# A softcap attention and maxout kernel whose list of work is put in another order

## The chip, the cores and the metric

The kernel runs on one core of one Trainium2 chip. The metric is device time in microseconds (us). Before the change the median of three runs was 328.67 us, the lowest 328.39 and the highest 329.13.

## The reference

Attention with a soft cap on the scores, then a feed-forward layer whose activation is the larger of two products. Inputs and output are float32; batch 8, 12 heads, 448 positions, head size 64, so x has 3584 rows and 768 columns; the hidden width is 1024.

```
scores = scale * (q @ k.T)                 # scale = 1/8
scores = cap * tanh(scores / cap)          # cap = 30
attn   = softmax(scores)
x      = (attn @ v)  -> [3584, 768]
g      = maximum(x @ w1, x @ w2)           # [3584, 1024]
out    = g @ w_out                         # [3584, 768]
```

## The kernel before

**The algebra.** Since max(a, b) = relu(a - b) + b, the kernel forms wd = w1 - w2 (`subtract`, into `wd_sb`) and wm = w2 @ w_out (`turn_w2` and `premultiply`, into `wm_sb`), and computes out = relu(x @ wd) @ w_out + x @ wm. The exponent is taken without subtracting the maximum, which the cap bounds.

**The tiling.** Two heads make a pair i (48 of them), two pairs a quad t (24). Scores are made transposed, three tiles of 128 key positions per pair (`S i j`, two matmuls of 448 columns, one for each head, on 64 rows of the array), and the last 64 positions of all four heads of a quad together (`L t`). ScalarE makes tanh out of PSUM (`T`, `TL`, line 519 and 532) and then exp in SBUF (`E`, `EL`). DVE adds the tiles of exponentials (`A`, `B`); a matmul with ones makes the sums (`Y`), DVE turns and inverts them (`Y1` to `Y3`); `VL` and `V` are the products with v (32-column tiles, four at a time), `N` scales them into xT on DVE.

The layer after it is cut into 120 groups, each of one PSUM bank out of four: per batch eight groups x @ wd of six units of 448 columns (stage 1), and six or eight groups of the output, of 14 units of 384 columns (stage 2). Each unit has two halves of 64 rows, and `M x y n` runs n units of the row half 0 of group x beside row half 1 of group y: two different groups are in work at a time. `ev g` empties a bank on DVE (line 666 for stage 1, 702 for stage 2), `eva g` on ScalarE (line 700); `st` stores rows of the output from SyncE's queue.

**Hand-overs.** Where a group's next matmul is on the other row half than its last, both write the same bank. `H g` (DVE) or `Hs g` (SyncE) issues a nop that waits for the group's last matmul (line 654); the first matmul of the other half then waits for this nop. A change of half with no such step of its own gets no added dependency (lines 634 to 650).

**The loads.** q, k and v of later pairs come through the DMA queue that GpSimd (POOL) feeds, which casts to bf16. `lk i part` and `lq i` fill `kqs` (line 328), `lv t part` fills `vp` and `vl` (line 352). There are two buffers of each, so a load for quad t waits until the buffer of quad t-2 is free: for `kqs` until its transposition has landed, for `vp` and `vl` until the products `V` and `VL` of that quad have read them. For the first ten pairs TensorE transposes q and k (`X`, `Xh`, copied by `XC`, `XCh`); for quads 5 to 23 a DMA transposition on SyncE's queue does (`cr t`, line 475, into `qkT`, also two buffers). The first two pairs come in float32 on the queues of SyncE and ScalarE (`ld0`) and are cast there (`cd`). `lw1`, `lw2`, `lwo` load the weights, on POOL's queue too. `D bank n` are matmuls on constants that keep TensorE at work while nothing else is there.

**What sets the order.** No scheduler: one string, `ORDER` (lines 9 to 202), names every step, and the program issues them one after the other through the table `STEPS`. Each engine and each DMA queue takes its own steps in this order; semaphores carry the dependencies between them. So `ORDER` decides, for TensorE, ScalarE, DVE, POOL's queue and SyncE's queue at once, what stands behind what: a POOL load whose buffer is not free holds every load behind it, and an `Hs` stands behind a `cr` on SyncE if the list says so.

Of the kernel before, what the change touches and what calls it, by code (L numbers as in the profile page):

```python
# [9 lines left out]
ld0 q; ld0 q 1; cd q; ld0 k; ld0 k 1; ms; dm; ms0; cd k; id; lq 2 0; lk 3 0; lq 3 0; lk 2 0; lw2 3; lw2 2; D 3 24;  # L10
Xh 0 0 0; Xh 0 1; cd k 1 1; cd q 1 1; XCh 0 1; XCh 0 0; D 3 4; X 1 1; S 0 0; S 0 1; XC 1; T 0 0; T 0 1; D 0 5;
D 1 8; D 3 1; D 1 4; S 0 2; D 1 4; L 0; D 1 16; T 0 2; TL 0; E 0 0 3; D 1 12; S 1 2; S 1 0; X 3 3; X 2 0; W 3 2;
W 2 1; T 1 0; T 1 2; lw2 1; lwo 0 0; lwo 0 1; lw2 0; lq 4 0; lk 4 0; lv 0 0; lv 0 1; XC 3; XC 2; WC 3; D 0 4;
S 1 1; D 0 8; D 2 2; S 2 1; W 1 2; WC 2; WC 1; T 1 1; T 2 1; S 2 0; D 0 4; L 1; OP 3 0 0; P 3 0 2; OP 1 0 1;
P 1 0 4; P 3 0 2; OP 2 0 3; P 2 0 7; P 1 0 1; P 2 0 1; P 1 0 1; P 3 0 2; P 1 0 2; PC 2 0; PC 1 0; E 1 2 3;
E 1 0 2; TL 1; T 2 0; EL 0; S 3 0; S 2 2; P 3 0 1; W 0 2; P 3 0 1; X 4 3; T 2 2; T 3 0; VL 0; Y 0 1; V 0 0 0 3;
V 0 1 0 3; S 3 1; lwo 1 0; lwo 1 1; lq 5 0; lk 5 0; lv 1 0; lv 1 1; lk 8 0; lq 8 0; lq 7 0; lw2 4; lv 6 2; lq 6 0;
lk 7 0; lk 6 0; lw2 5; lw1 2; lw1 4; lw1 0; lv 2 0; lv 2 1; WC 0; PC 3 0; XC 4; Y1 0; Y2 0; Y3 0; N 0 0; N 0 1;
E 2 0 3; T 3 1; EL 1; E 3 0 2; OP 0 0 1; P 0 0 2; OP 2 1 2; P 2 1 2; P 0 0 1; OP 1 1 3; P 1 1 2; P 0 0 1; P 1 1 2;
P 0 0 1; P 1 1 4; S 4 0; S 3 2; X 5 0; P 2 1 4; P 0 0 3; P 2 1 1; XC 5; PC 1 1; PC 0 0; T 3 2; T 4 0; E 3 2 3;  # L20
OP 3 1 3; P 3 1 1; P 2 1 1; S 4 1; S 4 2; Y 1 1; T 4 1; T 4 2; L 2; P 3 1 4; VL 1; TL 2; V 1 1 0 3; V 1 0 0 3;
S 5 0; X 6 0; E 4 0 3; T 5 0; EL 2; Y1 1; Y2 1; PC 2 1; Y3 1; N 1 1; N 1 0; XC 6; X 7 2; W 4 1; S 5 2; S 5 1;
X 8 0; P 3 1 3; WC 4; XC 8; PC 3 1; T 5 1; T 5 2; OP 4 0 1; P 4 0 2; OP 0 1 0; P 0 1 3; S 6 0; S 6 1; W 5 3;
P 0 1 1; P 4 0 6; P 0 1 4; E 5 0 2; T 6 1; T 6 0; E 5 2 3; XC 7; sub 2 0; WC 5; sub 4 0; PC 4 0; sub 0 0; PC 0 1;
OP 5 1 3; P 5 1 4; S 6 2; L 3; Y 2 1; T 6 2; TL 3; E 6 0 3; VL 2; V 2 1 0 1; V 2 0 0 3; V 2 1 1 3; S 7 0; P 5 1 4;
OP 5 0 0; P 5 0 8; Y1 2; Y2 2; Y3 2; N 2 0; N 2 1; A 3 0 1; A 3 0 2; PC 5 1; PC 5 0; T 7 0; EL 3; lk 9 0; lq 11 0;
lv 3 1; lq 9 0; lw1 1; lw1 3; lq 10 0; lk 12 1; lv 3 0; lw1 5; lk 10 0; lk 11 0; lk 11 1; lk 10 1; S 7 2; O 0 1;
M 0 -1 2; S 7 1; M 0 -1 4; O 1 2; M 1 -1 1; T 7 2; T 7 1; Hs 0; M 1 -1 1; S 8 1; M 1 -1 1; M 1 0 3; S 8 0; X 9 3;
OP 4 1 0; P 4 1 4; sub 1 0; sub 3 0; XC 9; T 8 1; E 7 0 2; T 8 0; E 7 2 3; P 4 1 4; L 4; O 2 3; M 2 0 3; S 8 2;
M 2 1 3; A 3 1 1; B 3 1; PC 4 1; ev 0; B 3 0; Hs 2; TL 4; T 8 2; O 3 0; M 3 1 3; M 3 2 1; S 9 0; M 3 2 2; T 9 0;  # L30
E 8 0 3; ev 1; A 3 1 2; sub 5 0; cr 5; Hs 3; O 4 1; M 4 2 1; VL 3; V 3 0 0 3; Y 3 2; V 3 1 0 3; M 4 2 2; S 9 1;
M 4 3 3; lk 13 0; lk 13 1; lv 4 1; lv 4 0; lv 5 3; lv 5 0; lq 13 0; lq 15 0; lq 12 0; lk 12 0; lk 15 1; Y1 3;
Y2 3; Y3 3; ev 2; Hs 4; O 5 2; M 5 3 3; M 5 4 3; T 9 1; EL 4; ev 3; N 3 0; N 3 1; Hs 5; O 6 3; M 6 4 3; M 6 5 2;
S 10 0; M 6 5 1; O 7 0; M 7 5 3; Hs 6; ev 4; A 4 0 1; ev 5; M 7 6 2; S 9 2; M 7 6 1; Hs 7; cr 6; E 9 0 2; T 10 0;
T 9 2; O 8 1; M 8 6 3; S 10 2; M 8 7 3; S 10 1; O 9 2; M 9 7 1; T 10 2; T 10 1; E 9 2 3; M 9 7 2; VL 4; V 4 0 0 2;
L 5; TL 5; A 4 1 1; H 8; A 4 0 2; B 4 1; ev 7; B 4 0; A 4 1 2; ev 6; M 9 8 3; V 4 1 0 3; Y 4 0; V 4 0 2 3;
# [169 lines left out]
def kernel(  # L206
# [21 lines left out]
    P = 128  # L228
# [550 lines left out]
```

## Time and profile before

| what | value |
|---|---|
| median of the runs | 328.67 us |
| span of the profiled execution | 326.9 us |
| TensorE busy | 320.2 us, 98% |
| ScalarE busy | 281.1 us, 86% |
| DVE busy | 240.1 us, 73% |
| POOL busy | 162.2 us, 50% |
| matmuls | 4138 |
| longest single waits of POOL's loads: for a transposition / for scores of TensorE | 6.3 us / 9.5 us |

The profile is of one execution, and its span stands 1.8 us under the median of the runs, which contains what lies around it. PE is TensorE, PEld its loading of weights, ACT ScalarE, DVE VectorE, SP SyncE; a q behind the name means the engine's queue of instructions. The share of busy time is a mean over unlike stages: a head of about 56 us in which the weights are prepared and the first quads start, a long middle, and a tail from about 286 us in which only groups of the last batches remain. In the slices each digit is the busy share of one fortieth of the span, in tenths.

### The profile page before, as it was taken

Reading aid. Unit: us, or ns where it says so; the run is one execution under the profiler, and the core shown is the slowest. Engines: PE = TensorE matmul, PEld = TensorE weight load, DVE = VectorE, ACT = ScalarE, POOL = GpSimd, SP = SyncE. Lnnn points to the kernel's source line nnn. Section 1 sums busy time; section 2 is a strip of 40 time slices with the busy share of each in tenths; the row PEclk is TensorE's granted clock in tenths of the full one; section 3 lists DMA queues with packets and bytes.
Section 4 is the critical chain, followed back from the end, with each engine's and each line's share of the span. In section 5 each row is a group of like instructions: output and inputs, shape, how many; then the busy total and the mean of one; then the engine's idle time right before and its main releaser. Section 6 shows DMA issues by size and latency. Waiting matters only on the chain.

```text
span 326.9 us, 9772 instructions
## 1 busy us (share of the span) xinstructions
PE 320.2 (98%) x4138; PEld 184.5 (56%) x4138; DVE 240.1 (73%) x422; ACT 281.1 (86%) x278; POOL 162.2 (50%) x237
## 2 busy tenths in 40 slices
PE   7999999999999999999999999999999999999994
PEld 3454545545656664565565565556466556557662
DVE  3346899987997778987897788968878779773201
ACT  5999999999999999999999999999999999921120
POOL 7357584568772772764774474478448311000000
PEclk9999999999999999999999999999999999999999
DMA  8999999899999999999999999999999963013033
GB/s 179 174 202 185 269 256 112 92 140 116 221 188 98 134 182 191 102 99 175 163 176 108 208 114 181 128 140 182 183 116 101 201 156 45 2 50 98 0 98 96
DMA packets 134508, 46.28 MB, mean 142 GB/s; under 512 B 112321, under 2 KB 129473, under 8 KB 134465
## 3 DMA queue, kind: packets, MB, share of 16 engines
q0 software_dynamic: 94592, 25.02, 78.3%
q1 hardware_dynamic: 39424, 19.99, 31.1%
q8 instruction: 32, 0.52, 0.6%
q10 hardware_dynamic: 448, 0.66, 0.5%
q14 instruction: 12, 0.09, 0.1%
HBM read 47.78 MB, written 11.01 MB: 180 GB/s over the span
## 4 chain that ended last, share of the span: by engine, by line
PE 93%; DMA 3%; POOL 1%; DVE 1%; issue 0%
PE mm L645 61%; PE s L514 9%; PE s L606 9%; PE mm L431 5%; DMA w2b<-in_moe_w_dram 3%; PE s L528 2%; PE s L600 2%; PE mm L573 2%; PE mm L640 1%; POOL kqs L321 1%; PE mm L458 1%; PE mm L566 1%; PE mm L416 0%; DVE xT L621 0%; POOL w2b L366 0%; DVE xT L618 0%
## 5 line engine op out<-in xcount | busy, mean ns | idle before, releaser
L519 ACT ACTIVATE e<-s 128x896 bf16<-128x896 f32 x144 | 125.5, 927 | 5.7 <-PE s L514 5.2
L536 ACT ACTIVATE e<-e 128x1792 bf16<-128x1792 bf16 (+2 forms) x72 | 122.7, 1709 | 0.0
L645 PE MATMUL mm<-wo_sb,gT 64*128 64x384 bf16 x864 | 115.2, 323 | 0.0
L645 PE MATMUL mm<-wm_sb,xT 64*128 64x384 bf16 x648 | 102.2, 323 | 0.0
L645 PE MATMUL mm<-xT,wd_sb 64*128 64x448 bf16 x768 | 97.5, 349 | 0.0
L328 POOL DMA_DIRECT2D kqs<-in_k_dram x76 | 54.7, 722 | 56.1 <-DMA qkT<-kqs 50.9
L645 PEld LDWEIGHTS <-gT 64*128 64x128 bf16 x864 | 58.6, 94 | 25.5 <-issue 1.1
L645 PEld LDWEIGHTS <-wd_sb 64*128 64x128 bf16 x768 | 48.8, 94 | 26.7 <-issue 2.1
L645 PEld LDWEIGHTS <-xT 64*128 64x128 bf16 x648 | 50.3, 94 | 18.5 <-issue 0.2
L514 PE MATMUL s<-qkT 64*128 64x448 bf16 x288 | 52.7, 352 | 0.2 <-DVE xT L618 0.2
L352 POOL DMA_DIRECT2D vp<-in_v_dram x48 | 30.5, 639 | 32.6 <-PE s L514 23.5
L666 DVE TENSOR_SCALAR gT<-mm 128x448 bf16<-128x448 f32 x64 | 38.9, 617 | 8.7 <-PE mm L645 7.6
L328 POOL DMA_DIRECT2D kqs<-in_q_dram x38 | 35.1, 924 | 5.7 <-issue 2.5
L606 PE MATMUL s<-e,vp 128*32 128x448 bf16 x576 | 36.1, 354 | 0.0
L548 DVE TENSOR_TENSOR esum<-e 128x896 bf16<-128x896 bf16 x42 | 25.9, 617 | 9.1 <-ACT e L536 9.1
L621 DVE TENSOR_TENSOR xT<-s,inv 64x448 bf16<-64x448 f32 x48 | 29.9, 622 | 1.7 <-PE s L606 0.8
L548 DVE TENSOR_TENSOR esum<-esum,e 128x896 bf16<-128x896 bf16 x42 | 26.2, 623 | 5.9 <-ACT e L536 4.8
L514 PEld LDWEIGHTS <-qkT 64*128 64x128 bf16 x288 | 18.5, 94 | 20.1 <-issue 12.0
L700 ACT COPY osb<-mm 128x384 f32<-128x384 f32 x10 | 4.8, 479 | 26.9 <-PE mm L645 26.7
L702 DVE COPY osb<-mm 128x384 f32<-128x384 f32 x44 | 23.3, 554 | 6.2 <-PE mm L645 5.7
L553 DVE TENSOR_TENSOR esum<-esum,el 64x896 bf16<-64x896 bf16 x42 | 26.0, 619 | 1.2
L578 DVE STREAM_TRANSPOSE st<-mm 128x448 f32<-128x448 f32 x24 | 15.6, 649 | 13.0 <-PE mm L573 11.3
(57 smaller groups left out, 269.7 us busy)
## 6 DMA issues: line engine op xcount, KB each, us to landing
out_dram<-osb SPq DMA_DIRECT2D x54, 192.0 KB, 4.5
vp<-in_v_dram POOLq DMA_DIRECT2D x38, 160.0 KB, 4.3
kqs<-in_q_dram POOLq DMA_DIRECT2D x46, 112.0 KB, 5.8
kqs<-in_k_dram POOLq DMA_DIRECT2D x76, 56.0 KB, 4.4
osb<-in_moe_w_dram POOLq DMA_DIRECT2D x4, 512.0 KB, 7.4
w2b<-in_moe_w_dram POOLq DMA_DIRECT2D x6, 256.0 KB, 7.1
wo_sb<-in_moe_w_out_dram POOLq DMA_DIRECT2D x4, 384.0 KB, 9.9
vp<-in_v_dram POOLq DMA_DIRECT2D x10, 128.0 KB, 7.7
```

The source lines that it names most:

```text
L328: nc.gpsimd.dma_start(out=to, in_=x)
L352: nc.gpsimd.dma_start(out=to, in_=x)
L514: scored[i, j] = nc.tensor.matmul(s[:, h, :S], k_of(t, o, h, j), q_of(t, o, h)).ins
L519: nc.scalar.activation(expo[i][:, 2 * j : 2 * j + 2, :], slots[i, j][:, :, :S], AF.Tanh, scale=scale / cap)
L536: nc.scalar.activation(e, e, AF.Exp, scale=float(cap))
L548: nc.vector.tensor_add(d, e[:, 0:2, :] if j == 1 else d, e[:, 2 * j : 2 * j + 2, :])
L553: nc.vector.tensor_add(d, d, left_e[t][r, :, :])
L606: nc.tensor.matmul(vals[t][place(m, u), u, :S], w[:, m, :], expo[2 * t + o][:, 2 * j + h, :], start=False, stop=(j == NJ - 1))
L621: nc.vector.tensor_mul(x[64 - r : 128 - r], vals[t][r : r + 64, u, :S], sums[t, 3][64 - r : 128 - r])
L645: ins = nc.tensor.matmul(self.ps, w[r], x[r], start=first, stop=self.at == [self.n, self.n]).ins
L666: nc.vector.tensor_relu(gT[b // 2][:, f, cs], ps)
L702: nc.vector.tensor_copy(o[:, hs], ps)
```

## The change

Nothing but the order and the place of a few steps changes, and one condition in `transposes`. Every score, exponential, load, transposition and group unit of the old list is in the new one. In the new list:

- every one of the 145 changes of row half has a hand-over of its own: 63 are `H` (21 before), 82 `Hs` (107 before). Before, 17 changes had none (among them those of groups 1, 10, 12, 17, 24, 27, 40, 42, 47, 54, 57);
- of the evictions, 118 are `ev` and 2 `eva` (26 and 29); before, 110 and 10 (100 to 103 and 112 to 117);
- the loads of a quad are mixed with those of its neighbours and lie at other distances from their use; on POOL's queue the head now begins with `lk 2`, `lq 2`, and `lwo 0 0`, `lwo 0 1` come ahead of `lw2 1`;
- the first loads bring pair 1 ahead of pair 0, and of pair 0 q is transposed ahead of k;
- products for wm and group units are cut into smaller pieces: 81 steps `P` instead of 36, 772 steps `M` instead of 746, with the same number of matmuls.

The list is ten lines longer, so every line of the code below it has a number higher by ten.

```diff
-ld0 q; ld0 q 1; cd q; ld0 k; ld0 k 1; ms; dm; ms0; cd k; id; lq 2 0; lk 3 0; lq 3 0; lk 2 0; lw2 3; lw2 2; D 3 24;
-Xh 0 0 0; Xh 0 1; cd k 1 1; cd q 1 1; XCh 0 1; XCh 0 0; D 3 4; X 1 1; S 0 0; S 0 1; XC 1; T 0 0; T 0 1; D 0 5;
+ld0 q 1; ld0 q; ld0 k 1; ld0 k; ms0; dm; D 0 24; lk 2 0; lq 2 0; cd q; id; lq 3 0; cd k; Xh 0 1 0; cd q 1 1;
+lw2 3; Xh 0 0; XCh 0 1; cd k 1 1; D 1 4; lw2 2; XCh 0 0; S 0 0; lk 3 0; S 0 1; T 0 0; D 0 8; lwo 0 0; X 1 3;
...
+cr 6; O 7 0; M 7 5 1; H 6; ev 3; M 7 5 2; E 9 0 2; M 7 6 1; A 4 0 1; M 7 6 2; O 8 3; M 8 6 1; ev 5; M 8 6 1;
...
+T 10 2; M 9 8 2; lk 16 0;
...
+lq 16 0; Y 4 0; V 4 1 0 3; Y1 4; lk 15 0; ... lv 5 3; ... lk 16 1; ... lq 14 0; ... lq 15 0; ... lk 14 1;
...
+M 12 10 1; M 12 11 1; lk 17 0; M 12 11 1; H 10; S 12 0; cr 7; S 12 1; M 12 11 1; M 10 11 1; T 12 0; M 10 11 1;
...
+M 14 13 1; EL 6; lk 19 0; S 13 2; S 13 1; H 14; M 12 13 2; lv 6 0; M 12 13 1; T 13 2; M 12 13 3; lv 7 3;
+M 12 13 2; T 13 1; S 14 1; ev 12; O 15 0; M 15 13 1; lv 6 1;
...
+V 18 1 0 2; ev 75; Y 18 3; V 18 0 0 2; E 38 0 3; Y1 18; V 18 0 2 3; V 18 1 2 3; M 77 76 1; Y2 18; lv 20 1;
+M 77 76 1; Y3 18; M 77 76 1; O 78 2; M 78 76 1; lk 42 1; M 78 76 1; Hs 77; M 78 76 1; N 18 0; S 39 0; M 78 77 1;
...
+lv 20 3; S 39 2; M 80 78 1; M 80 79 1; cr 21; T 39 2; M 80 79 1; ev 78; M 80 79 1; O 81 1; M 81 79 1; S 40 0;
+H 80; A 19 0 1; E 39 0 2; M 81 79 2; M 81 80 1; A 19 0 2; M 81 80 2; S 40 1; ev 79; O 82 2; M 82 80 1; Hs 81;
...
+L 20; lq 47 0; VL 19; TL 20; V 19 0 0 2; A 19 1 2; V 19 1 0 2; lq 45 0; V 19 0 2 3; ... lv 20 0; ... lk 44 0;
+ ... lq 44 0; ... lv 20 2; ... lk 45 0; ...
+M 86 85 1; lk 47 1; H 84; A 20 1 1; M 86 85 2; cr 22; M 84 85 2; B 20 1; T 42 1; lv 21 0; M 84 85 1; S 42 2;
+M 84 85 1; B 20 0; M 84 85 1; lv 21 1; M 84 85 1; T 42 2; M 84 85 1; A 20 0 2; M 84 85 1; Hs 86; O 87 2;
+M 87 85 1; lv 21 2; M 87 85 2; E 41 2 3; M 87 86 1;
...
     def transposes(i, bank, c=None):
 
-        if c != 1:
+        if bank is not None:
             turned["qk", i] = mm_tile(bank).bitcast(bf16)
         ps = turned["qk", i]
```

The condition lets whichever half of pair 0 comes first take the PSUM bank.

More of the change, by code (lines that the diff above doesn't have):

```diff
@@ L15 @@
[L15 to L24, printed above, removed]
@@ L200 @@
-O 118 1; M 118 118 1; eva 117; M 118 118 6; st 7 5; M 118 118 7; O 119 2; M 119 119 2; ev 118; M 119 119 12;
-ev 119; st 7 6;
+ld0 q 1; ld0 q; ld0 k 1; ld0 k; ms0; dm; D 0 24; lk 2 0; lq 2 0; cd q; id; lq 3 0; cd k; Xh 0 1 0; cd q 1 1;
+lw2 3; Xh 0 0; XCh 0 1; cd k 1 1; D 1 4; lw2 2; XCh 0 0; S 0 0; lk 3 0; S 0 1; T 0 0; D 0 8; lwo 0 0; X 1 3;
+T 0 1; lwo 0 1; S 0 2; XC 1; D 1 5; T 0 2; lw2 1; L 0; X 2 3; TL 0; lw2 0; S 1 2; XC 2; lq 4 0; D 2 4; T 1 2;
+S 1 0; lk 4 0; D 1 1; D 2 8; T 1 0; D 1 2; lv 0 0; D 2 4; D 3 16; lv 0 1; EL 0; lwo 1 0; S 2 1; E 0 0 3; S 1 1;
@@ new lines @@
+W 3 0; lwo 1 1; W 2 3; WC 3; D 1 4; lk 5 0; ms; X 3 0; lq 6 0; D 2 12; T 1 1; lk 6 0; WC 2; lq 5 0; OP 3 0 1;
+P 3 0 1; XC 3; OP 2 0 2; P 2 0 1; T 2 1; P 3 0 2; lv 1 1; D 0 4; P 3 0 1; E 1 0 2; lv 1 0; L 1; S 2 0; lw1 2;
+P 2 0 1; P 3 0 1; P 2 0 2; P 3 0 1; lq 7 0; E 1 2 3; P 2 0 1; P 3 0 1; P 2 0 1; lw2 4; P 2 0 1; P 3 0 1; TL 1;
+lk 7 0; Y 0 0; Y1 0; lw2 5; T 2 0; S 3 0; lw1 4; PC 3 0; W 1 3; T 3 0; S 2 2; lw1 0; WC 1; P 2 0 1; W 0 1;
+T 2 2; PC 2 0; lw1 1; OP 1 0 3; P 1 0 2; WC 0; P 1 0 1; EL 1; P 1 0 1; lw1 5; P 1 0 3; OP 0 0 2; P 0 0 1;
@@ new lines @@
+M 15 13 1; lv 6 1; M 15 13 2; T 14 1; A 6 0 1; M 15 14 1; lq 19 0; S 14 0; M 15 14 1; ev 13; M 15 14 1; T 14 0;
+O 16 2; M 16 14 1; A 6 0 2; M 16 14 1; Hs 15; lq 18 0; M 16 14 1; M 16 15 1; E 13 0 2; M 16 15 1; ev 14;
+M 16 15 1; O 17 3; M 17 15 1; lv 7 0; M 17 15 1; Hs 16; cr 8; M 17 15 1; M 17 16 1; S 14 2; ev 15; M 17 16 2;
+T 14 2; A 6 1 1; O 18 1; M 18 16 3; Hs 17; B 6 0; E 13 2 3; L 7; VL 6; B 6 1; V 6 0 0 2; lv 8 3; TL 7;
+V 6 1 0 2; A 6 1 2; V 6 0 2 3; V 6 1 2 3; ev 16; Y 6 0; EL 7; lv 8 0; S 15 0; Y1 6; M 18 17 2; lv 7 1;
@@ new lines @@
+Y3 20; M 87 86 4; N 20 1; T 43 0; M 87 86 1; O 88 0; M 88 86 2; Hs 87; st 5 3; M 88 86 1; M 88 87 1; EL 21;
+M 88 87 1; S 43 1; H 86; M 88 87 1; N 20 0; M 86 87 2; T 43 1; M 86 87 1; H 88; ev 84; M 86 87 1; S 43 2;
+M 86 87 2; st 5 4; T 43 2; M 86 87 2; O 89 1; M 89 87 2; ev 86; M 89 87 1; E 43 0 2; M 89 88 2; A 21 0 1;
+M 89 88 1; cr 23; M 89 88 1; S 44 1; ev 87; S 44 0; M 89 88 2; A 21 0 2; M 89 88 1; T 44 0; M 89 88 3; st 5 5;
+M 89 88 1; O 90 3; M 90 88 1; T 44 1; M 90 88 1; H 89; A 21 1 1; M 90 88 1; M 90 89 1; S 44 2; E 43 2 3;
@@ new lines @@
+M 90 89 1; Hs 88; M 90 89 1; M 88 89 2; H 90; M 88 89 1; T 44 2; M 88 89 1; A 21 1 2; M 88 89 4; O 91 2;
+M 91 89 1; E 44 0 3; M 91 89 1; ev 88; M 91 89 1; M 91 90 2; ev 89; M 91 90 1; O 92 0; M 92 90 1; B 21 0;
+M 92 90 2; H 91; L 22; ev 90; VL 21; V 21 0 0 2; TL 22; lv 23 2; B 21 1; V 21 0 2 3; V 21 1 0 2; A 22 0 1;
+lv 22 2; Y 21 3; EL 22; V 21 1 2 3; Y1 21; lv 23 3; S 45 0; M 92 91 2; T 45 0; M 92 91 1; lv 22 0; Y2 21;
+O 93 3; M 93 91 1; Y3 21; M 93 91 1; Hs 92; M 93 91 1; lv 23 0; M 93 92 1; S 45 1; ev 91; M 93 92 1; lv 23 1;
@@ new lines @@
+M 99 97 2; H 98; M 99 98 2; ev 97; M 99 98 3; ev 96; M 99 98 1; VL 22; B 22 1; L 23; V 22 1 0 2; TL 23;
+V 22 1 2 3; Y 22 0; V 22 0 0 2; Y1 22; V 22 0 2 3; EL 23; M 99 98 1; S 47 0; Y2 22; M 99 98 1; A 23 0 1;
+M 99 98 1; T 47 0; M 99 98 2; O 100 3; M 100 98 1; Y3 22; M 100 98 1; Hs 99; M 100 98 1; M 100 99 1; S 47 1;
+N 22 0; Hs 98; M 100 99 2; T 47 1; M 98 99 2; H 100; N 22 1; M 98 99 3; E 47 0 2; M 98 99 3; O 101 0;
+M 101 99 3; M 101 100 1; S 47 2; ev 99; M 101 100 2; T 47 2; M 101 100 1; ev 98; M 101 100 2; A 23 0 2;
@@ new lines @@
+M 101 100 3; E 47 2 3; M 101 100 1; A 23 1 1; M 101 100 1; O 102 1; M 102 100 2; H 101; M 102 100 1; B 23 0;
+M 102 101 2; Hs 100; st 5 6; M 102 101 1; B 23 1; M 100 101 3; A 23 1 2; M 100 101 4; Hs 102; M 100 101 1;
+VL 23; Y 23 2; V 23 0 0 2; Y1 23; V 23 1 0 2; V 23 1 2 3; Y2 23; V 23 0 2 3; ev 100; O 103 2; M 103 101 3;
+Y3 23; M 103 102 4; N 23 0; M 103 102 3; N 23 1; M 103 102 4; O 104 3; M 104 102 2; Hs 103; M 104 102 1;
+M 104 103 1; ev 101; M 104 103 1; Hs 102; M 104 103 1; st 6 1; M 102 103 2; H 104; M 102 103 6; O 105 0;
@@ L202 @@
+M -1 117 1; M 116 117 2; ev 115; M 116 117 3; st 7 4; M 116 117 3; M -1 117 2; ev 116; M -1 117 1; O 118 2;
+M 118 118 1; ev 117; M 118 118 3; st 7 5; M 118 118 10; O 119 1; M 119 119 2; ev 118; M 119 119 12; ev 119;
+st 7 6;
 """
```

335 lines of the change are left out of this document (157 added, 178 removed).

## The prediction

> **What bounds the kernel now.** I read the page's busy times and slices first, then the chain that ended last, then the same engines stage by stage, and last the waits of each queue.
>
> ```profile
> span 326.9 us, 9772 instructions
> PE 320.2 (98%) x4138; PEld 184.5 (56%) x4138; DVE 240.1 (73%) x422; ACT 281.1 (86%) x278; POOL 162.2 (50%) x237
> PE   7999999999999999999999999999999999999994
> ACT  5999999999999999999999999999999999921120
> PEclk9999999999999999999999999999999999999999
> PE 93%; DMA 3%; POOL 1%; DVE 1%; issue 0%
> ```
>
> TensorE is busy 98% of the span, at full clock, and makes 93% of the chain. ScalarE is as full until 286 us. What differs by stage:
>
> ```profile
> 8.00:20.00 12.00, 11.46 (x142) 6.05 (x142) 3.30 (x6) 12.00 (x13) 4.57 (x8) 1.00 1.18 181
> 20.00:32.00 12.00, 11.98 (x181) 6.16 (x178) 7.72 (x15) 11.47 (x12) 8.15 (x14) 1.00 1.28 192
> 44.00:56.00 12.00, 12.00 (x145) 6.27 (x143) 11.64 (x20) 12.00 (x13) 7.92 (x12) 1.00 1.26 171
> 104.00:128.00 24.00, 24.00 (x322) 14.02 (x320) 19.12 (x36) 23.68 (x23) 14.25 (x20) 1.00 1.24 137
> 300.00:327.00 27.00, 22.78 (x236) 14.39 (x232) 4.24 (x7) 2.88 (x6) 0.00 (x0) 0.98 0.27 72
> ```
>
> These are stretches of the trace: after each length come busy us and instructions of PE, PEld, DVE, ACT, POOL. Until 56 us ScalarE is full but for 0.53 us: the head goes by it. From there to the tail TensorE is full, so a list with the same matmuls can win only gaps shorter than these columns show, and lose whatever makes TensorE stand. The recorded waits say that today almost nothing does:
>
> ```profile
> POOL kqs L328 <- DMA qkT<-kqs: 52.5, 14, 6.3
> POOL vp L352 <- PE s L514: 23.5, 6, 9.5
> ACT e L519 <- PE s L514: 5.2, 9, 0.8
> SPq L654 <- PE mm L645: 218.7, 103, 48.0
> SPq L475 <- DMA kqs<-in_k_dram: 4.4, 1, 4.4
> ```
>
> The load queue (POOL) waits for the DMA transpositions (14 times, 52.5 us), that is, it stands ready before its buffers are free. SyncE waits for TensorE; only once (4.4 us) did a transposition wait for a k load. So loads are early now. That earliness is what the change spends.
>
> **The change part by part.** Both lists hold the same steps, counted by kind: 1177 group units, 144 scores, 72 exponentials, 19 transpositions, every load. Matmuls stay 4138. What differs is order, the kind of hand-over and a few eviction engines.
>
> *Loads of one quad* (two pairs of heads). They come later on the list (distances are the matmuls between two steps, at the prices given below). From a quad's last v load to its left-over values there were 16.6 to 19.5 us of TensorE work (from quad 7 on); after, it is 4.8 to 7.8 us in ten or so quads (6, 7, 8, 9, 11, 13, 17 to 20, 22). From the last k or q load to the transposition it was some 12 us; after, 2.6 to 3.9 us in quads 7, 9, 13, 21 and 22. The prices:
>
> ```profile
> L328 POOL DMA_DIRECT2D kqs<-in_k_dram x76: 702/716/772, 43.6 to 250.1; - x76
> L328 POOL DMA_DIRECT2D kqs<-in_q_dram x38: 912/922/957, 36.1 to 250.8; - x38
> DMA to landing us min/median/max: 2.4/4.8/9.1
> L352 POOL DMA_DIRECT2D vp<-in_v_dram x48: 617/640/667, 11.6 to 268.7; - x48
> DMA to landing us min/median/max: 2.7/4.3/10.1
> L475 SPq DMA_TRANSPOSE qkT<-kqs x19: 1296/1655/2655, 55.3 to 262.6; - x19
> DMA to landing us min/median/max: 4.2/6.7/10.0
> kqs<-in_k_dram POOLq DMA_DIRECT2D x76, 56.0 KB, 4.4
> ```
>
> A k load takes the queue 0.72 us, a q load 0.92, a v load 0.64 or 0.62; they land 4.4 (k) and 4.3 us (v) after issue. A transposition occupies SyncE for 1.66 us and lands after 6.7. TensorE's work is priced from the chain:
>
> ```profile
> 139.27 2.60 PE mm L645 x32
> 166.88 1.14 PE mm L645 x12
> 160.42 0.87 PE s L606 x16
> ```
>
> One stage-2 pair is 2.60/16 = 0.1625 us, one stage-1 pair 1.14/6 = 0.19 (a score pair has the same 448 columns: 0.19), a mixed pair between them 0.176, one 32-column matmul of the values 0.87/16 = 0.054 (I use it for left-overs and sums too).
>
> Tightest place, quad 22 and group 86. The last value matmul of quad 18 frees the v buffer; call that 0. Then in order: `lv 20 1` (0.64) on POOL, `lk 42 1` lands 4.4 later (5.04), `cr 21` lands 6.7 later (11.74). Now `lq 47 0`, which writes the buffer that `cr 21` reads, is at the head of POOL's queue; behind it stand `lq 45`, `lv 20 0`, `lk 44 0`, `lq 44`, `lv 20 2` and `lk 45 0`. The six ahead of `lk 45 0` take 3 x 0.92 + 0.72 + 0.64 + 0.62 = 4.74 (16.48), it lands at 20.88, `cr 22` occupies SyncE to 22.5, and `Hs 86`, a hand-over that `M 87 86` needs, is next on SyncE. TensorE has between: 56 stage-2 pairs (9.1), 27 stage-1 (5.1), 9 mixed (1.6), 12 scores (2.3), 44 narrow matmuls (2.4): 20.5 us. So it stands **2.0 us**. (`Hs 81` behind `cr 21`, free at 6.7, is needed at about 6.6 to 6.8 and lies inside this.) In the old list the loads of quad 22 lie next to one another, and no hand-over stands right behind `cr 21` or `cr 22`.
>
> Second place, quads 6 and 7. From `cr 6`: landing 6.7; `lk 16 0`, `lq 16`, `lk 15 0`, `lv 5 3`, `lk 16 1`, `lq 14`, `lq 15` take 3 x 0.72 + 3 x 0.92 + 0.62 = 5.54; `lk 14 1` lands 4.4 later (16.64), `cr 7` 6.7 later (23.34). The first score of quad 7, `S 14 1`, is due about there (some 22 us of work and its gaps): no charge. But `lk 19 0` waits for `cr 7`; then `lv 6 0`, `lv 7 3`, `lv 6 1` issue at 23.34 + 0.72 + 0.64 + 0.62 = 25.32, landing at 29.6. `V 6` is due after 75 stage-2 pairs (12.2), 18 mixed (3.2), 24 stage-1 (4.6), 14 scores (2.7) and 104 narrow (5.6) = 28.3. **1.3 us.** Its follower, `cr 8`, `lk 21 0`, `lk 20 0`, `lk 18 1`, `lv 7 2`, `lk 19 1`, `cr 9`, `S 18 0`: 6.7 + 2.78 + 4.4 + 6.7 = 20.6 against 39 x 0.1625 + 9 x 0.176 + 28 x 0.19 + 10 x 0.19 + 88 x 0.054 = 19.9 plus the 1.3 already lost: none. The other shortened distances (4.8 us or more from a load to its use, against landings of 4.3 to 4.4) are covered.
>
> Bounds: with the shortest landings (2.4 a load, 4.2 a transposition) the first place needs 0.64 + 2.4 + 4.2 + 4.74 + 2.4 + 1.66 = 16.0, the second is free: 0. With the longest (9.1, 10.0) the first needs 35.2, 14.7 us too many. I take the medians, since the DMA share in these stretches is that of the whole kernel (1.24 above).
>
> [...]
>
> *Head.* The first loads now bring pair 1 ahead of pair 0, and the first scores want pair 0:
>
> ```profile
> 4.24 0.56 ACT L308 CAST kqs<-qr 128x448 bf16<-128x448 f32 x1 [1.28 <-DMA qr<-in_q_dram]
> 5.47 0.56 ACT L308 CAST kqs<-qr 128x448 bf16<-128x448 f32 x1
> 6.82 2.53 ACT L519 ACTIVATE e<-s 128x896 bf16<-128x896 f32 x3 [0.80 <-PE s L514]
> 15.20 0.62 PE L416 MATMUL mm<-ident,w2b 128*128 128x128 bf16 x8 [0.52 <-DMA w2b<-in_moe_w_dram]
> ```
>
> Pair 0's q is cast at 4.24 as soon as it lands; as the second load of its queue it lands perhaps half an issue of 0.89/2 later, and `lk 2`, `lq 2` now run beside it. The first tanh moves from 6.82 by 0 to 1.0 us; I take **+0.4**, because ScalarE behind it is full to 56 us. In return w2 is asked for a load earlier and two parts of w_out come ahead of `lw2 1`; the wait at 15.20 is 0.52 us and lies under ScalarE's row of 12.00, so nothing is credited. Seven warming steps carry the same 96 units; real work before the last of them is 4.64 us and 4.67.
>
> *Hand-overs.* 145 half changes in both; 17 had no nop of their own and now have one. DVE's go from 21 to 63, SyncE's from 107 to 82.
>
> ```profile
> L654 SPq EVENT_SEMAPHORE  x107: 17/17/17, 49.6 to 315.9; - x107
> L654 DVEq EVENT_SEMAPHORE  x21: 21/21/21, 64.5 to 299.6; - x21
> ```
>
> 42 x 21 ns is 0.9 us of an engine that is idle for 87; what stands behind such a nop on DVE (evictions, sums) waits until TensorE ends a half. The shortest distance, three pairs (0.49 us), is that of the old list. I take 0; ends 0 and +1.0.
>
> *Evictions.* Ten on ScalarE at the tail become ordinary DVE ones; two (26 and 29) go to ScalarE in mid-kernel.
>
> ```profile
> L700 ACT COPY osb<-mm 128x384 f32<-128x384 f32 x10 | 4.8, 479 | 26.9 <-PE mm L645 26.7
> L702 DVE COPY osb<-mm 128x384 f32<-128x384 f32 x44 | 23.3, 554 | 6.2 <-PE mm L645 5.7
> ```
>
> The tail's 8 x 0.55 us lie on a DVE with 4.24 us busy in its last 27; the two on ScalarE cost 0.96 us of an engine that is full 23.68 of 24, beside a TensorE that is full 24.00. 0; end +1.0.
>
> *Switches of tile shape.* 131 become 129; at about 0.1 us each (the row at 160.42 and its neighbours leave gaps of that size) **-0.2**. Finer interleaving (772 group steps for 746) is order only: 0.
>
> Sum: 2.0 + 1.3 + 0.4 - 0.2 = **+3.5 us**. The profiled execution spans 326.9, and 1.8 us lie around it to the median of 328.67; 326.9 + 3.5 + 1.8 = **332.2 us**, 1.1% slower. What can be told from no change is 0.2%.
>
> **The rivals.**
>
> (a) *The loads land in time, and the head gains*: faster. Place: the two queues above and the w2 wait at 15.20. With k loads below 3.4 us in both of its positions the first place is even (2 x 1.0 = 2.0); isolated ones may do so:
>
> ```profile
> 105.01 0.72 POOL L328 DMA_DIRECT2D kqs<-in_k_dram  x1 [5.88 <-DMA qkT<-kqs]
> 116.44 0.70 POOL L328 DMA_DIRECT2D kqs<-in_k_dram  x1 [4.31 <-DMA qkT<-kqs]
> ```
>
> Loads that go out like these, alone after a wait of some 5 us, are where I look for the smallest landing of 2.4 us. Both critical loads come right behind others, which speaks against. Then what is left is -0.2 and a first product sooner by the 0.52 us of that wait and the issue of one load (0.61 to 0.71): 328.67 - 1.4 = 327.3. [...]
>
> (b) *The list only deals the same work anew*: the late loads are just covered, head and switches cancel: 328.5. For it: 4138 matmuls and a full TensorE; against: two chains that come out over.
>
> (c) *One late load makes the next late.* `lq 47 0`, `lk 19 0` wait at the head of an in-order queue, and what stands behind waits with them; SyncE's hand-overs stand behind `cr`. With one landing of 9.1 or 10.0 us in each place, 4 to 5 us more: about 337.
>
> **How the numbers follow.** The forecast 0.45, its own range 329.4 to 334.5; (a) 0.25; (b) 0.08; (c) 0.22, which starts where the forecast's range ends. Low: 326.3, a microsecond under (a) for gaps I cannot see; high: 338, (c) and an end of a nop or eviction. Faster 0.25, same 0.08, slower 0.67.
>
> **What the changed kernel should show.** TensorE waits for POOL's loads or SyncE: about 2 us before `M 87 86` (near 255 us) with SyncE's transposition row waiting for k loads several times, not once; about 1.3 us before `V 6` (near 92 us) on a v load. The first tanh after 6.82. ScalarE's evictions two, DVE hand-overs 63. If the rows of k loads waiting on transpositions shrink and TensorE's busy share is still 98%, my landing times were too long, and (a) holds. A group's eviction held behind a DVE hand-over, or ScalarE idle in the middle, would be a cause that I charged nothing.

## The result: slower by 5.7%, and the profile after

The changed kernel takes 347.2 us at the median (346.0 to 348.6), the kernel before 328.5: a ratio of 1.057, 95% interval 1.054 to 1.061. The forecast was 332.2 with an upper end of 338. Medians, ranges and ratios here leave out executions that took over 1.5% longer than the fastest of their kernel, and the profiled one of the changed kernel, 351.2 us, is one of these. A stand described below (before `V 18`) is in its profile and not in every one.

The page of the profile after, with the lines that answer to those of before:

```profile
span 349.1 us, 9772 instructions
...
PE 328.4 (94%) x4135; PEld 189.0 (54%) x4138; DVE 243.3 (70%) x430; ACT 280.4 (80%) x270; POOL 162.9 (47%) x237
PE   6999599999999899899899999999699999999995
...
ACT  3899749999999899989989999999679999930000
...
PEclk9999969999999999999999999999899999999999
...
PE 79%; DMA 12%; DVE 2%; POOL 2%; issue 1%; ACT 1%; SPq 1%; ACTq 0%; POOLq 0%; DVEq 0%
```

TensorE's slices were 9 from the second to the last but one; now one is 5 and one 6, and in the slice behind the first of them the clock is 6. TensorE makes 79% of the chain instead of 93%, and DMA 12% instead of 3%: it waits for loads now. Three stretches of the changed kernel (after the length: busy us and instructions of PE, PEld, DVE, ACT, POOL; then the granted clock, the load of the DMA engines and GB/s):

```profile
32.00:44.00 12.00, 7.91 (x137) 3.89 (x135) 7.06 (x12) 9.36 (x9) 4.42 (x7) 0.95 1.12 285
44.00:56.00 12.00, 11.93 (x108) 6.51 (x112) 8.00 (x10) 7.25 (x8) 6.26 (x9) 0.76 0.64 48
248.00:272.00 24.00, 21.18 (x254) 11.81 (x256) 16.02 (x29) 19.25 (x19) 13.17 (x18) 0.93 1.16 136
```

Its waits, by engine and releaser (total us, times, longest):

```profile
PEld L655 <- SPq L664: 6.2, 8, 1.7
PE mm L468 <- DMA kqs<-in_q_dram: 3.8, 1, 3.8
PE s L616 <- DMA vp<-in_v_dram: 3.3, 1, 3.3
PE mm L655 <- SPq L664: 2.8, 4, 1.3
SPq L485 <- DMA kqs<-in_k_dram: 14.3, 8, 4.6
```

Three causes stand here: a q load before a transposition of the head (L468), a v load before the values (L616), and the hand-overs of SyncE (L664). Before, no row of TensorE's waits named SyncE, and its waits for loads were of 0.3 to 0.8 us. Transpositions waited for k loads eight times (14.3 us) instead of once.

To put the time to places I matched every matmul of a trace with its step on the list and took, for each step, its start minus the priced work ahead of it (prices of the prediction, the same for every kernel). The growth of this difference is the time lost in a stretch of the list; us in the profiled executions:

| priced work on TensorE | before | after | e1 | e9 | e14 |
|---|---|---|---|---|---|
| 0 to 10 us | 1.8 | 5.9 | 5.3 | 4.6 | 4.3 |
| 10 to 41 | 1.7 | 8.5 | 2.1 | 2.1 | 2.1 |
| 41 to 91 | 1.8 | 3.7 | 4.1 | 3.3 | 3.4 |
| 91 to 151 | 1.8 | 6.4 | 6.2 | 4.0 | 2.1 |
| 151 to 222 | 2.0 | 7.5 | 2.1 | 2.1 | 2.1 |
| 222 to 302 | 1.9 | 2.1 | 2.8 | 2.8 | 1.9 |

e1, e9 and e14 are the experiments below, which take the causes away one after the other. The 7.5 us of the changed kernel between 151 and 222 us hold the stand before `V 18`.

### The profile page after: what moved, and what is told of

It is laid out like the page before. It is cut to its first block, busy times and chain, and to the rows that moved or that the text cites. A ratio compares the mean times of both kernels' runs of the same rounds, so it can differ in the third digit from the quotient of the medians.

```text
span 349.1 us, 9772 instructions
## 1 busy us (share of the span) xinstructions
PE 328.4 (94%) x4135; PEld 189.0 (54%) x4138; DVE 243.3 (70%) x430; ACT 280.4 (80%) x270; POOL 162.9 (47%) x237
## 4 chain that ended last, share of the span: by engine, by line
PE 79%; DMA 12%; DVE 2%; POOL 2%; issue 1%; ACT 1%; SPq 1%; ACTq 0%; POOLq 0%; DVEq 0%
PE mm L655 52%; PE s L616 8%; PE s L524 8%; DMA kqs<-in_q_dram 4%; DMA qkT<-kqs 2%; PE mm L441 2%; DMA osb<-in_moe_w_dram 2%; DMA vp<-in_v_dram 2%; PE mm L583 2%; PE s L538 2%; PE mm L650 1%; PE mm L468 1%; PE s L610 1%; DMA qr<-in_q_dram 1%; PE mm L481 1%
## 5 line engine op out<-in xcount | busy, mean ns | idle before, releaser
L655 PE MATMUL mm<-xT,wd_sb 64*128 64x448 bf16 x768 | 100.6, 351 | 2.6 <-SPq L664 2.5
L655 PEld LDWEIGHTS <-wd_sb 64*128 64x128 bf16 x768 | 50.6, 94 | 31.0 <-SPq L664 5.0
L524 PE MATMUL s<-qkT 64*128 64x448 bf16 x288 | 54.9, 358 | 1.0 <-DVE qkT L473 0.5
L712 DVE COPY osb<-mm 128x384 f32<-128x384 f32 x52 | 28.2, 552 | 22.3 <-PE mm L655 21.9
L362 POOL DMA_DIRECT2D vl<-in_v_dram x38 | 23.7, 626 | 38.8 <-PE s L610 27.6
L616 PE MATMUL s<-e,vp 128*32 128x448 bf16 x576 | 34.5, 361 | 4.7 <-DMA vp<-in_v_dram 3.3
L524 PEld LDWEIGHTS <-qkT 64*128 64x128 bf16 x288 | 17.8, 94 | 17.0 <-issue 6.0
```

Source lines behind the costliest of these rows:

```text
L362: nc.gpsimd.dma_start(out=to, in_=x)
L524: scored[i, j] = nc.tensor.matmul(s[:, h, :S], k_of(t, o, h, j), q_of(t, o, h)).ins
L616: nc.tensor.matmul(vals[t][place(m, u), u, :S], w[:, m, :], expo[2 * t + o][:, 2 * j + h, :], start=False, stop=(j == NJ - 1))
L655: ins = nc.tensor.matmul(self.ps, w[r], x[r], start=first, stop=self.at == [self.n, self.n]).ins
L712: nc.vector.tensor_copy(o[:, hs], ps)
```

## The experiments

**One load ahead of its time.** The largest loss, 8.5 us between 10 and 41 us of work, is this piece of the chain and this row of TensorE's time line:

```profile
36.64 7.29 DMA kqs<-in_q_dram
```

```profile
44.07 0.95 PE L468 MATMUL mm<-ident,kqs 64*64 64x64 bf16 x28 [3.84 <-DMA kqs<-in_q_dram]
```

The row is `X 7 0`, the transposition of pair 7. The load of the chain is `lq 10`. The two share a buffer, `kqs[1]`: pairs 6 and 7 lie in it one behind the other, but from pair 10 on a q load writes every second block of 64 columns, and `lq 10` so covers half of what pair 7 has there. On the old list `lq 10` comes behind `X 7`. On the new one it comes 27 steps ahead, so `X 7 0` must wait for its landing, and turns a mixture of both pairs: by the list and the addresses in `load`, the changed kernel computes the scores of pair 7 from partly foreign data, and so changes more than the order. The data that `X 7` should read had been asked for at 25.4 and 26.5 us.

```diff
-Y3 1; lq 10 0; E 4 0 3; ...
+Y3 1; E 4 0 3; ...
-X 7 0; T 5 2; ...
+X 7 0; lq 10 0; T 5 2; ...
```

> The changed kernel with one step moved: `lq 10 0` stands right behind `X 7 0` instead of 27 steps ahead of it. (In the changed list `lq 10` writes half of the 64-column blocks of the buffer in which pair 7 still waits for its transposition, so that `X 7 0` has to wait for the landing of `lq 10` and turns a mixture of both pairs; here pair 7 is turned from its own data.) Theory: this order alone makes the longest stand of TensorE in the head, 3.84 us before `X 7 0`, and the stand lowers the clock, which was 0.95 and 0.76 in the two stretches of 12 us around it (0.6 and 2.9 us lost). It should win 3.8 + 3 = about 6.5 us of the 347.2: 340.7. Rival: the head waits for the weights and loads that are in flight anyway, and the stand only moves to the next transposition or the next scores: 345 to 347.

Measured: 339.8 us, ratio to before 1.037 (1.033 to 1.041): 7.4 us won between the medians. The page and the stretch behind the place, with this one edit:

```profile
span 337.7 us, 9775 instructions
...
PEclk9999999999999999999999999999999999999999
```

```profile
44.00:56.00 12.00, 11.73 (x155) 5.77 (x154) 10.91 (x16) 11.81 (x12) 6.05 (x10) 1.00 0.68 55
```

The stand, the lowered clock and ScalarE's empty time (7.25 busy before the edit, 11.81 with it) go together. The theory holds, and the rival falls: nothing else in the head was about to make TensorE wait as long.

**Is it the stand that lowers the clock?**

```diff
-sub 2 0; X 7 0;
+sub 2 0; D 0 64; X 7 0;
```

> The changed kernel with 16 dummy matmuls of 512 columns (3.4 us at full clock) put ahead of `X 7 0`, that is, into the stand of 3.84 us, which itself remains. Theory: the standing of TensorE lowers the clock; with the dummies the granted clock stays at 1.00 in 44 to 56 us and some 3 us are won: 344. Rival: the clock drops for another reason (the DMA load or the mix of matmuls in this stretch): 347, and the stretch still shows 0.76.

The stretches of this kernel:

```profile
32.00:44.00 12.00, 10.65 (x148) 4.88 (x146) 7.07 (x12) 8.54 (x8) 4.02 (x7) 1.00 1.12 286
44.00:56.00 12.00, 11.48 (x122) 6.00 (x122) 9.39 (x13) 9.30 (x11) 6.29 (x9) 1.00 0.64 48
```

With the dummies in it the same wait leaves the clock at 1.00, at the same DMA load (1.12, 0.64). So the standing lowers it here. In the changed kernel the granted clock is 0.50 from 43 to 49.5 us; the stand of 3.84 us ends at 44.07. It fell behind shorter stands too: 3.26 us here (0.93 above) and 2.56 us in e13, below (0.72). Behind 2.41 us in e12 the next 24 value matmuls took 1.32 us, the price of the prediction (0.054 us each). The length of a stand alone does not settle it: in e8 the clock was 0.87 from 8 to 20 us, and no matmul of that trace waits longer than 2.0 us. In time the edit showed nothing: 348.0 us (345.5 to 348.2), ratio 1.057 (1.053 to 1.062). The 3 us stay a reading of the trace, not a measured gain.

**One v load.** In the profiled execution the values of quad 18 stood 3.3 us. The chain there:

```profile
229.76 8.64 DMA qkT<-kqs
...
238.93 0.72 POOL kqs L338
...
243.03 7.65 DMA vp<-in_v_dram
...
250.82 0.76 PE s L616 x8
```

`cr 19` lands after 8.64 us; only then can the load go that heads POOL's queue (`lk 43 1`), and `lv 18 1`, five loads behind it, is issued at 243.03 and lands after 7.65 us.

```diff
-lv 18 0; M 71 70 3; ...
+lv 18 0; lv 18 1; M 71 70 3; ...
-M 73 72 2; lv 18 1; O 74 3; ...
+M 73 72 2; O 74 3; ...
```

> The changed kernel with one load moved: `lv 18 1` right behind `lv 18 0`, that is, ahead of the loads that wait for the DMA transposition `cr 19`. Theory: the stand of 3.3 us before `V 18` is made by this one load, issued at 243.0 us because it stands behind six loads of which the first waits for `cr 19`, and landing only after 7.7 us because `cr 20` is on its way; with it goes the lowered clock behind the stand (0.93 in 248 to 272 us, 1.7 us). 347.2 - 5 = 342.2. Rival, the place of the prediction: behind it the chain `cr 21`, `lq 47 0`, `cr 22`, `Hs 86` comes too late as well, it was only covered by this stand, and takes 2 us back: 344.

Measured: 347.7 us, ratio 1.059 (1.055 to 1.063), nothing won. The stand is absent from this kernel's profile, but from that of e1 as well, where the load was not moved. My reading of one profile was no theory of the median.

Laid side by side, the traces show when the stand comes. In the changed kernel's profile, in e10 and in e12, `cr 20` went out on SyncE 0.8 to 1.5 us ahead of `lv 18 1` on POOL; the load then took 7.65, 9.32 and 6.85 us, and `V 18` stood 3.3, 3.6 and 1.8 us. In e1, e2, e6 to e9 and e11 the load went out first, by 0.01 to 1.05 us, took 3.9 to 5.3 us, and `V 18` did not stand. Two queues race here, and the list does not say which one wins. No run sets this order alone, so this is a reading of ten traces; and not every load behind a transposition is slow (`lv 13 1` behind `cr 15` took 4.5 us in e11 and 4.9 in e12).

**The hand-overs alone.** The old list with the 17 missing ones:

```diff
-M 1 -1 1; M 1 0 3; S 8 0;
+M 1 -1 1; M 1 0 3; Hs 1; S 8 0;
```

> The kernel before with nothing added but the 17 missing hand-overs (on SyncE's queue, each right behind the last unit of the first row half), so that every one of the 145 changes of row half has its own: this part of the change alone. Theory: they lie 2.3 us or more ahead of their use and cost nothing, 328.5 within 0.4. Rival: each wait on TensorE costs some 0.1 us as a switch does, or is caught behind a transposition on SyncE: 330 to 331.

Measured: 329.1 us, ratio 1.0024 (1.0015 to 1.0034). So a hand-over at every change costs 0.8 us by itself: between theory and rival, and little of the 18.7.

**Three edits behind e1.** The first loads in the old order, 15 hand-overs from SyncE to DVE, and one scaling step behind the values.

```diff
-ld0 q 1; ld0 q; ld0 k 1; ld0 k;
+ld0 q; ld0 q 1; ld0 k; ld0 k 1;
```

> The changed kernel with `lq 10` behind `X 7` (339.8 us as measured), and besides with the first loads in the old order: pair 0 ahead of pair 1, for q and for k. Theory: the first transposition starts at 5.86 instead of 4.50 us because pair 0's q lands as the second load of its queue (cast at 5.29 instead of 4.24); put first, it starts about 1.0 us sooner, and since ScalarE is what the head goes by, the whole is 1.0 sooner: 338.8. Rival: the head's 3.5 us are lost behind it, by transpositions and dummy matmuls that stand ahead of the scores, and nothing comes of it: 339.8.

Measured: 340.3 us, ratio 1.039 (1.034 to 1.044): no gain. In the trace the first transposition does start at 4.8 instead of 5.9 us, and by 41 us of work 1.0 us is still won; later stands behind SyncE took it back.

The second edit rests on these rows of the changed kernel's chain:

```profile
146.66 1.04 SPq L485
...
147.75 0.02 SPq L664
...
172.99 1.71 SPq L485
...
174.75 0.02 SPq L664
```

SyncE is issuing a transposition (L485), and the nop of a hand-over (L664), which waits for nothing else by then, comes behind it.

```diff
-cr 12; H 34; ... Hs 35; st 1 5; ... Hs 36; st 1 3;
+cr 12; H 34; ... H 35; st 1 5; ... H 36; st 1 3;
```

> The changed kernel with `lq 10` behind `X 7`, and besides with the 14 hand-overs that stand next behind a DMA transposition on SyncE's queue, and `Hs 36`, issued by DVE instead. Theory: SyncE is held 1.3 to 2.9 us by issuing a transposition (0.5 to 0.9 by a store), and the hand-over behind it makes TensorE stand: 0.7 before `M 3 2`, 1.1 and 0.7 before `M 36 35` and `M 37 36`, 1.0 behind `M 46 45`, some tenths elsewhere. Some 3.2 us are won: 336.6. Rival: on DVE these nops hold back evictions and sums, and what is won is given back: 339 to 341.

Measured: 338.3 us, ratio 1.030 (1.026 to 1.034): 1.5 us between the medians, about half of what was expected, and the interval just touches that of e1. In the trace the waits of TensorE's matmuls for SyncE fall from 2.9 to 1.7 us, and one of 1.6 us for a transposition is new.

```diff
-V 7 0 0 2; lv 8 1; N 7 1; V 7 0 2 3;
+V 7 0 0 2; lv 8 1; V 7 0 2 3; N 7 1;
```

> The changed kernel with `lq 10` behind `X 7`, and besides with `N 7 1` behind `V 7 0 2 3` instead of ahead of it. Theory: as the list stands, the last values of quad 7 wait for both halves of the scaling `N 7 1` on DVE (0.62 + 0.64 us), a stand of 1.5 us before `V 7 0 2 3` that no other quad has; 338.3. Rival: TensorE is ahead of the loads and of ScalarE there, and the time goes to the next wait: 339.8.

Measured: 342.4 us, ratio 1.043 (1.040 to 1.046), 2.6 us slower than e1 by the medians, though the intervals just touch. The wait for `N 7 1` in e1 and what SyncE's hand-overs cost there, and then the same rows of e8, in which the first kind has no row any more:

```profile
PE s L616 <- DVE xT L631: 1.4, 1, 1.4
PEld L655 <- SPq L664: 6.3, 8, 1.4
PE mm L655 <- SPq L664: 2.9, 4, 0.9
```

```profile
PEld L655 <- SPq L664: 10.3, 10, 2.0
PE mm L655 <- SPq L664: 6.2, 9, 1.5
```

The stand before `V 7 0 2 3` is gone (1.4 us), and TensorE then waits 3.3 us longer for SyncE. What the step is worth by itself cannot be told from this run; that it only makes TensorE arrive earlier at the next late nop is what the rows suggest.

The three at once:

> The three edits together with `lq 10` behind `X 7`: first loads in the old order, 15 hand-overs on DVE, `N 7 1` behind `V 7 0 2 3`. Theory, their sum: 339.8 - 1.0 - 3.2 - 1.5 = 334.1; what would be left to the kernel before is then the head's order and about a microsecond of hand-overs. Rival: one list's stands cover one another, half comes back: 337.

Measured: 336.5 us, ratio 1.025 (1.021 to 1.028); 3.3 us of the 5.7 expected. What is left behind SyncE is one row of its queue, here from the issue of `cr 12` on, and TensorE's wait at its end:

```profile
135.70 2.86 SPq L485 DMA_TRANSPOSE qkT<-kqs  x1
138.61 1.59 SPq L691 DMA_DIRECT2D out_dram<-osb  x2
140.25 0.60 SPq L686 DMA_DIRECT2D out_dram<-osb  x1
140.90 0.91 SPq L687 DMA_DIRECT2D out_dram<-osb  x1
```

```profile
141.91 0.36 PE L655 MATMUL mm<-xT,wd_sb 64*128 64x448 bf16 x1 [1.63 <-SPq L664]
```

A transposition and two stores hold SyncE for 6 us without a gap, and `Hs 37` comes after them.

**All hand-overs on DVE, and the head.**

```diff
-M 38 36 2; Hs 37; M 38 37 1;
+M 38 36 2; H 37; M 38 37 1;
```

> The kernel of the three edits (336.5 us), with all 82 hand-overs that SyncE still issues moved to DVE. Theory: what is left of stands in its middle lies before `M 38 37` (1.8 us, behind a transposition of 2.86 us and two stores of 1.5 us each on SyncE), `M 88 89` (1.0) and at the start of the groups (0.8): 336.5 - 3 = 333.5. Rival: DVE, busy 72%, is held by the nops that wait for TensorE, and its evictions and sums come late: 336 to 340.

Measured: 334.4 us (332.6 to 335.0), ratio 1.017 (1.013 to 1.021): 2.1 us won by the 67 hand-overs that SyncE had left. If DVE was held by them, it cost less than that.

```diff
-XCh 0 0; S 0 0; ... T 0 0; D 0 8; lwo 0 0; X 1 3; ... S 0 2; XC 1;
+XCh 0 0; X 1 3; S 0 0; ... T 0 0; XC 1; D 0 8; lwo 0 0; ... S 0 2;
```

> The kernel of the three edits, with the head as in the old list in one point: the transposition of pair 1 (`X 1`) ahead of the first scores, where TensorE waits 0.54 us for a copy, instead of between the second and the third score tile; the copy `XC 1` follows. Theory: of the 4.6 us that TensorE has lost by 10 us of its work (1.8 in the kernel before) some 1.2 come from this place, and ScalarE, which the head goes by, starts its third tanh a microsecond sooner: 335.4. Rival: the head's loss is given back where ScalarE has room (11.0 of 12 us in 32 to 44): 336.5.

> Both of these together: 336.5 - 3 - 1.1 = 332.4 by the theory, 336 or more by the rivals. The kernel before stays faster in either case: 328.5.

Measured: 336.9 us (ratio 1.026, 1.022 to 1.031) and 336.2 us (1.024, 1.021 to 1.027), neither better than without the edit of the head; the second is 1.8 us slower than the kernel that it was made from. In the trace of the second the first 10 us of work lose 0.7 us less than in e9, but its TensorE stands at late v loads:

```profile
95.82 1.32 PE L616 MATMUL s<-e,vp 128*32 128x448 bf16 x24 [2.41 <-DMA vp<-in_v_dram]
238.65 0.56 PE L616 MATMUL s<-e,vp 128*32 128x448 bf16 x8 [1.81 <-DMA vp<-in_v_dram]
```

These are `V 6` and `V 18`, and in both places the v load went out behind a transposition.

**The same cost put into the kernel before.** Its 21 DVE hand-overs are not scattered: 20 of them come next behind a transposition on the list, singly or in twos. Here all are on SyncE.

```diff
-... cr 21; ... H 83; ... H 82 2;
+... cr 21; ... Hs 83; ... Hs 82 2;
```

> The kernel before with its 21 DVE hand-overs issued by SyncE instead. 20 of them stand next behind a DMA transposition on the list, which is where the changed list has 14 on SyncE. Theory: the place of a hand-over behind a transposition on SyncE costs TensorE time in the old list too, some 0.2 to 0.3 us for each of the 17 transpositions concerned (their issue takes 1.3 to 2.7 us): 328.5 + 4 = 332.5. Rival: a hand-over costs nothing wherever it stands, and the stands of the changed list come from its late transpositions alone: 328.5 to 329.

Measured: 337.3 us, ratio 1.028 (1.024 to 1.033): 9.0 us, more than twice the expected. TensorE's longest wait in this kernel, and then the stretch behind it:

```profile
69.02 1.14 PE L645 MATMUL mm<-wm_sb,xT 64*128 64x384 bf16 x5 [2.56 <-SPq L654]
```

```profile
68.00:80.00 12.00, 10.98 (x103) 5.12 (x105) 5.56 (x11) 6.53 (x7) 7.53 (x11) 0.72 1.00 110
```

The nop's place costs twice: the stand, and the clock behind it (0.72, that is 3.4 of the 12 us). What stood ahead of the nop was `cr 6`, which itself waited for a k load and went out only at 67.41 us:

```profile
SPq L475 <- DMA kqs<-in_k_dram: 4.3, 1, 4.3
```

So the nop paid for the wait of the transposition as well as for its issue (1.50 us). This place makes some 6 of the 9 us; TensorE's other four waits for SyncE come to 3.1 us, and no wait for a late transposition has a row. This is the clearest single result: a hand-over of 17 ns is dear where a transposition is ahead of it in its queue, above all one that is not ready.

**Late v loads.** In the old list each v load of quads 7 to 23 comes within 27 steps of the last value step of quad t-2, which frees the buffer; in the changed list up to some 135 steps behind it. In e14 all v loads of quads 6 to 23 go back to right behind that reader.

```diff
-V 16 0 2 3; Y2 16; ...
+V 16 0 2 3; lv 18 0; lv 18 1; Y2 16; ...
```

> The kernel with the three edits and all hand-overs on DVE (334.7 us), and besides with every v load of quads 6 to 23 put as early as its buffer allows, right behind the last reader of quad t-2, which is where the old list has them (within 27 steps; the changed list has them up to 139 steps behind). Theory: the stands before `V 6`, `V 13` and `V 18` are late v loads, they come and go from run to run, and with them goes the lowered clock behind them; median 332, spread under 2 us, and what is left to the kernel before, 3 us, lies in the head. Rival: the v loads now stand ahead of k and q loads on POOL's queue, whose transpositions come later, and the stands move to the scores: 334 to 337.

Measured: 333.1 us (331.5 to 333.4), ratio 1.012 (1.010 to 1.015): 1.3 us between the medians, with intervals that just overlap. In the trace no v load makes TensorE stand. Its page:

```profile
span 331.1 us, 9795 instructions
...
PE 322.5 (97%) x4138; PEld 187.3 (57%) x4138; DVE 242.8 (73%) x430; ACT 279.1 (84%) x270; POOL 162.4 (49%) x237
```

In the table above e14 loses 4.0 us between 151 and 302 us of work, the kernel before 3.9. What it loses more lies ahead of 91 us: 9.8 against 5.3. No experiment takes that away: the first loads stand in the old order here already, and the place of `X 1` accounts for 0.7 us in the trace of e12 and for nothing in the medians.

Last, the hand-overs behind stores in the old list:

```diff
-O 14 3; M 14 12 2; EL 6; Hs 13; S 13 1;
+O 14 3; M 14 12 2; EL 6; H 13; S 13 1;
```

> The kernel before with 20 of its SyncE hand-overs, those next behind a store on the list, issued by DVE. Theory: a store holds SyncE 0.5 to 0.9 us, and in the old list such hand-overs still cost some tenths in all: 328.4 - 0.5 = 327.9. Rival: they lie far enough ahead of their use, 328.4; or DVE loses by them, 329.

Measured: 328.6 us, ratio 0.9999 (0.9988 to 1.0009). The hand-overs behind stores cost the old list nothing. No kernel here beats the one before.

## Why the prediction was wrong

The sign was right, the size was not: 3.5 us were forecast and 18.7 measured. Two steps failed above all. Of the loads only the distance to their use was priced, not whether the buffer's last reader came first (`lq 10`), and the hand-overs were taken at nothing. Step by step the experiments win back 7.4 us (e1), 3.3 (e9), 2.1 (e10) and 1.3 (e14); 4.5 us remain.

**"Loads of one quad", first place (2.0 us before `M 87 86`): mis-sized.** With the stand before `V 18` out of the way (e1), SyncE's queue shows both transpositions of that chain:

```profile
246.54 2.00 SPq L485 DMA_TRANSPOSE qkT<-kqs  x1
254.77 1.11 SPq L691 DMA_DIRECT2D out_dram<-osb  x2
260.93 1.76 SPq L485 DMA_TRANSPOSE qkT<-kqs  x1
```

From the issue of `cr 21` to SyncE's release behind `cr 22` are 16.2 us; I had 22.5 - 5.04 = 17.5. TensorE's weight load at 262.80 us waits 0.48 us for this nop, and in the changed kernel's own profile nothing waits there. The chain exists, with shorter landings.

**Second place (1.3 us before `V 6`): the mechanism was right, the size a matter of the execution.** From `cr 6` to the landing of `lv 6 1` I had 29.6 us; the changed kernel's profile has 28.6, and the load landed 0.1 us ahead of `V 6`, so nothing stood. In e12 `cr 8` went out ahead of `lv 6 1`, which then took 7.7 us instead of 4.9: 31.0 us in all, and a stand of 2.41. With the v loads put early (e14) the stand is gone.

**"The other shortened distances are covered": failed.** I set the distance on the list against a landing of 4.3 us. But a load does not go out where it stands on the list, it goes out when those ahead of it have (`lv 18 1` waited for `cr 19` and went out at 243.03 us), and the loads that went out beside a transposition took longer to land. Loads issued beside a transposition (and three stores) and loads issued without them, in two windows of the changed kernel:

```profile
kqs<-in_k_dram POOLq DMA_DIRECT2D x2, 56.0 KB, 7.8
vp<-in_v_dram POOLq DMA_DIRECT2D x1, 160.0 KB, 7.6
```

```profile
kqs<-in_k_dram POOLq DMA_DIRECT2D x3, 56.0 KB, 3.3
vp<-in_v_dram POOLq DMA_DIRECT2D x2, 160.0 KB, 3.5
```

The first are of 242 to 246 us, with `cr 20` on its way from 242.14; the second of 253 to 258. These are the ends of a range and not two fixed values. Of all q, k and v loads from `cr 5` on, the 61 that went out with a transposition on its way landed after 6.6 us in the median (2.6 to 8.3), the 117 others after 3.7 (2.0 to 8.1); the kernel before has 6.2 and 3.9. Stores are often on their way too, and no run takes the two apart.

**"Hand-overs: I take 0; ends 0 and +1.0": the step that failed in kind.** I priced the nop and looked at the distance to its use, not at what stands ahead of it in SyncE's queue, except at `Hs 81` and `Hs 86`. The old list showed the answer: 20 of its 21 DVE hand-overs are behind transpositions. Moving them alone costs 9.0 us (e13), most of it at one place; taking all hand-overs from SyncE in the changed list wins 1.5 us (e7) and, behind e9, a further 2.1 (e10).

**Not in the sum at all.** `lq 10` ahead of `X 7`, 7.4 us: I compared how far loads were from their uses, but did not ask of each load whether the buffer's last reader was still ahead of it. The scaling step ahead of the last values of quad 7, 1.4 us in the trace. And the clock: it fell behind the stands of 3.84, 3.26 and (in e13) 2.56 us, and 3.5, 1.7 and 3.4 us of full clock are missing in the stretches around them.

**"Head +0.4": mis-sized.** The first 10 us of work lose 5.9 us instead of 1.8. A microsecond of it is the order of the first loads. Part of the rest is that TensorE works slowly for longer, which these rows show, the first three of the changed kernel and the last of the one before:

```profile
5.90 0.95 PE L468 MATMUL mm<-ident,kqs 64*64 64x64 bf16 x28 [1.90 <-ACT kqs L318]
7.65 0.93 PE L524 MATMUL s<-qkT 64*128 64x448 bf16 x4 [0.25 <-DVE qkT L473]
12.00 0.66 PE L468 MATMUL mm<-ident,kqs 64*64 64x64 bf16 x28
6.42 0.55 PE L514 MATMUL s<-qkT 64*128 64x448 bf16 x4
```

Four score matmuls take 0.93 us at 7.65 us in the new list and 0.55 at 6.42 us in the old one; 28 transpositions of the new list take 0.95 us at 5.90 and 0.66 at 12.00. I counted the dummy matmuls as equal (96 units in both). But in the new list the first of them end at 4.01 us and TensorE then stands 1.90 us for a cast, while in the old list they end at 4.53 us, when the first transposition has begun. The page's clock reads full here, but the trace's first record of it is at 12.11 us (at 5.00 in the kernel before), behind the slow rows, and no run fills this stand, so what keeps TensorE slow is not shown, nor is it shown how much of the 5.9 us it makes.

Evictions and tile switches showed in no row and had no experiment of their own. Of the rivals, (a) and (b) fell with the result; (c), late loads that pile up behind heads of queues, was right in kind for `V 18` and for the hand-overs behind `cr`, which it named, but its places and most of the price were elsewhere.

## What to carry to other kernels

When a list is dealt anew, check each load against the last reader of its buffer before pricing any distance: a wrong order can be a wait, and wrong data, at once. Price a cheap instruction by the queue that it stands in: what the engine issues just ahead of it (here 1.3 to 2.9 us for a transposition), and what that one still waits for (4.3 us for a k load in e13), is its cost. Where two queues run side by side, ask which of their transfers goes out first, and price the load with the other one on its way too (here 6.6 us in the median against 3.7).

## What the runs showed of the hardware

Around a stand of TensorE of 3.84 us 3.5 us of full clock were lost (0.95 and 0.76 in two stretches of 12 us), around one of 2.56 us in e13 3.4 (0.72 in 12 us), around one of 3.26 us 1.7 (0.93 in 24 us). Behind one of 2.41 us in e12 24 value matmuls took 1.32 us, their price at full clock. In e8 the clock was 0.87 from 8 to 20 us, with no wait of a matmul above 2.0 us. With dummy matmuls in the first of these waits the clock stayed at 1.00 (e2). Issuing one DMA transposition held SyncE's queue for 1.3 to 2.9 us in the changed kernel. Its loads issued while a transposition was on its way landed after 6.6 us in the median, the others after 3.7.
